# Weight conversion cut into seven steps, 160 steps moved between VectorE and ScalarE, and the step list written anew

## The chip, the cores and the metric

The kernel runs on one core of a Trainium2 chip. The metric is the device time of one execution in microseconds. The kernel before takes 520.02 us, the median of three runs (519.7 to 520.5). Five engines matter: TensorE (PE; PEld is its weight load), VectorE (DVE), ScalarE (ACT), GpSimd (POOL), and SyncE (SP), which here only issues DMAs.

## The reference

A gated linear attention feeds a feed-forward layer with a squared ReLU:

```
B, H, S, D = 4, 8, 768, 48
for t in range(S):
    state = alpha[:, :, t, :, None] * state + einsum('bhd,bhe->bhde', k[:, :, t], v[:, :, t])
    y[:, :, t] = einsum('bhd,bhde->bhe', q[:, :, t], state)
x = y.transpose(0, 2, 1, 3).reshape(B * S, H * D)      # 3072 x 384
h = maximum(x @ w_in, 0)                               # w_in 384 x 2048
out = h * h @ w_out                                    # w_out 2048 x 384
```

The two weight matrices arrive as 64-bit floats, everything else as 32-bit floats. [...]

## The kernel before, in words

**Attention.** The sequence is cut into 24 blocks of 128 positions (6 chunks of 4 batches; block n is chunk n // 4 of batch n % 4). For each block the logarithm of alpha is summed along the positions by a matmul with a triangular matrix (steps `ln`, `log_high`, `log_rest`, `cs`), the sums are exponentiated (`eb`, `ei`), q and k are scaled by them (`mq`, `mk`), turned by TensorE (`qT`, `kT`; from block 4 on `turned_one`) and copied out of PSUM (`qc`, `kc`; from block 4 on `half_copied`, four to a block). Then come the scores (`sc`), the masked copy (`one_masked`), the sums for the state (`kv`), the state update on VectorE (`us`, `sa`, `sb`) and the output of two blocks at a time (`y_states`, `y_inner`, `yb`). Twelve copies of strips (`moved`) carry the output of two blocks to `xT`, the transposed input of the feed-forward layer.

**Feed-forward.** Four blocks make a group of 512 tokens, of which there are six. For the first group part of the first product is made with plain 32-bit matmuls (`ha`, `hb`, `hf`, with `ra`/`qa` and the like for ReLU and square). Everything else is made in three passes of a faster 32-bit format (fp32r): each operand is split into a high part and a rest (`split_x`, `rest_x`, `diff_x` for x; `cast_w`, `rest_w`, `diff_w` for weights; `split_h`, `rest_h`, `diff_h` for the hidden layer), and `in_x` and `in_y`, or `out_x` and `out_y`, multiply them. `out_plain` is the plain 32-bit form of the second product for a group's first pieces. Between the passes the accumulator is scaled (`in_scaled`, `out_scaled`), summed (`in_added`, `out_added`), rectified (`in_post`) and squared (`in_square`). A hidden piece has one of three kinds, A, M and D, which say how it is finished: kind D is finished by one VectorE instruction in `in_post`, kind A is squared on ScalarE, kind M on VectorE. Split weights that do not stay in SBUF are written to DRAM (`kept_l`, `kept_d`) and read back (`fetch`, 144 times).

**Weights.** The matrices are loaded and converted in 16 parts, parts 0 to 7 of `w_in` and 8 to 15 of `w_out`, each 128 x 768 values. A part is loaded by one DMA of 768 KB (`load_weights`, L395 and L399). `first` makes two VectorE instructions (exponent field, L422; upper mantissa bits, L426), `middle` two ScalarE instructions (exponent moved up, L435; lower word scaled, L438), `second` three VectorE instructions (sign, L444; mantissa joined, L448; product, L451).

**Order.** All of it is written out by hand as a list of words, `ORDER`, such as `ha:1` or `moved:0:3:2`. The program walks the list and issues each step's instructions. Each engine executes its own instructions in the order of the list; DMAs are issued in that order by SP, and a DMA that must wait holds up all later ones. Loads of the blocks 4 to 7 and of `w_in` also wait for the newest matmul listed ahead of them. `warm` is a matmul whose result is thrown away; there are 16. All matmuls are recorded at line L350, the ScalarE copies of `moved` at L779, the splits of x and of the hidden layer at L845, `in_scaled` at L898 and L900, `in_post` of kinds A and M at L923, `in_square` at L930 or, like other VectorE additions and products, at L802.

## Time and profile before

| | before |
|---|---|
| median of three runs | 520.02 us |
| profiled execution, its own time | 521.08 us |
| span of the profiled execution | 519.3 us |
| TensorE busy | 508.6 us, 5404 instructions |
| VectorE busy | 362.6 us, 629 instructions |
| ScalarE busy | 314.4 us, 681 instructions |
| HBM read and written | 88.10 MB and 17.33 MB |

The profiled execution takes 1.78 us more than its span, and 1.06 us more than the median. A busy share is an average over stages: what one stage is limited by is read from the stretch of time in which it lies. Instructions of one engine overlap a little at their ends, so that the busy time is less than the sum of the durations.

### The profile page before, as it was taken

What the parts mean: (1) busy time and instruction counts of PE and PEld (TensorE: products, weight loads), DVE (VectorE), ACT (ScalarE), POOL (GpSimd) and SP (SyncE); (2) the same over time, 40 slices, a digit from 0 to 9 for tenths busy, and PEclk for the clock granted to TensorE, in tenths of its full rate; (3) what the DMA queues carried; (4) which work ended last, traced back from release to release, by engine and by line L of the source; (5) the groups of instructions that cost most, each with busy time, mean ns of one, the idle gap of its engine ahead of it and who ended that gap; (6) DMA issues with size and microseconds to landing.
All of it is one profiled execution on the core that took longest, in us unless ns stands there. A gap on an engine that the chain in (4) does not pass through costs nothing.

```text
span 519.3 us, 13138 instructions
## 1 busy us (share of the span) xinstructions
PE 508.6 (98%) x5404; PEld 432.0 (83%) x5404; DVE 362.6 (70%) x629; ACT 314.4 (61%) x681; POOL 5.4 (1%) x29
## 2 busy tenths in 40 slices
PE   8989999999999999999999999999999999999997
PEld 6676788567778879987899988899987899988997
DVE  3678999998988898635998147597344598126961
ACT  4789999977486673058766247765253775324620
POOL 4000000000000000000000000000000000000000
PEclk9989999999999999999999999999999999999999
DMA  9969898977756668698876479756883744579301
GB/s 161 218 174 249 176 266 269 275 236 217 220 170 196 193 219 255 215 308 199 239 185 184 146 230 287 216 153 174 221 259 124 231 136 143 182 273 404 123 0 61
DMA packets 140762, 106.27 MB, mean 205 GB/s; under 512 B 109968, under 2 KB 113056, under 8 KB 140704
## 3 DMA queue, kind: packets, MB, share of 16 engines
q1 hardware_dynamic: 140704, 105.45, 70.1%
q8 instruction: 42, 0.69, 0.6%
q14 instruction: 16, 0.13, 0.1%
HBM read 88.10 MB, written 17.33 MB: 203 GB/s over the span
## 4 chain that ended last, share of the span: by engine, by line
PE 88%; DVE 4%; ACT 3%; DMA 2%; issue 1%; POOL 0%; DVEq 0%; ACTq 0%; POOLq 0%
PE o L350 40%; PE h L350 36%; PE sckv L350 4%; PE y L350 4%; PE cs L350 2%; PE T L350 2%; DMA a_in<-in_alpha_dram 1%; PE warm L350 1%; DMA q_in<-in_q_dram 1%; ACT x L779 1%; DVE hid L802 1%; DVE power L444 1%; DVE w_out L451 0%; DVE w_in L451 0%; DVE w_out L448 0%
## 5 line engine op out<-in xcount | busy, mean ns | idle before, releaser
L350 PE MATMUL h<-xa,wb 128*128 128x512 f32 x264 | 76.4, 397 | 0.8 <-ACT ks L754 0.6
L350 PE MATMUL h<-xl,wl 128*128 128x512 f32 x264 | 74.5, 390 | 0.0
L350 PE MATMUL h<-xd,wd 128*128 128x512 f32 x264 | 69.6, 397 | 0.0
L779 ACT COPY x<-y 32x256 f32<-32x256 f32 (+3 forms) x144 | 50.9, 366 | 16.9 <-PE y L350 14.6
L350 PEld LDWEIGHTS h<-xa,wb 128*128 128x128 f32 x264 | 48.8, 188 | 12.3 <-ACT ks L754 1.0
L350 PEld LDWEIGHTS h<-xl,wl 128*128 128x128 f32 x264 | 49.6, 188 | 11.0 <-DVE xl L848 0.2
L350 PEld LDWEIGHTS h<-xd,wd 128*128 128x128 f32 x264 | 48.7, 188 | 11.0 <-ACT h L900 0.5
L802 DVE TENSOR_TENSOR hid<-h,hid 128x512 f32<-128x512 f32 x44 | 29.7, 687 | 40.2 <-PE h L350 40.1
L350 PE MATMUL o<-wb,ha 128*128 128x384 f32 x168 | 56.9, 339 | 0.1
L350 PE MATMUL o<-wd,hd 128*128 128x384 f32 x320 | 56.9, 334 | 0.0
L350 PE MATMUL o<-wl,hl 128*128 128x384 f32 x168 | 56.2, 335 | 0.0
L350 PEld LDWEIGHTS o<-wd,hd 128*128 128x128 f32 x320 | 55.7, 188 | 0.3
L350 PE MATMUL o<-wb,hx 128*128 128x384 f32 x152 | 51.2, 337 | 0.0
L350 PE MATMUL o<-wl,hx 128*128 128x384 f32 x152 | 50.8, 334 | 0.0
L898 ACT ACTIVATE hid<-h 128x512 f32<-128x512 f32 x44 | 26.3, 598 | 38.8 <-PE h L350 38.7
L923 ACT ACTIVATE hid<-h 128x512 f32<-128x512 f32 x44 | 25.8, 598 | 36.4 <-PE h L350 36.1
L802 DVE TENSOR_TENSOR osb<-o,osb 128x384 f32<-128x384 f32 x24 | 12.9, 555 | 44.7 <-PE o L350 30.9
L350 PE MATMUL o<-w_out,hid 128*128 128x384 f32 x128 | 44.0, 491 | 0.0
L845 ACT ACTIVATE ha<-hid 128x512 fp32r<-128x512 f32 x42 | 26.1, 632 | 22.4 <-DVE hid L918 12.0
L900 ACT ACTIVATE h<-h 128x512 f32<-128x512 f32 x44 | 25.6, 591 | 22.8 <-PE h L350 22.6
L350 PEld LDWEIGHTS o<-w_out,hid 128*128 128x128 f32 x128 | 23.7, 189 | 15.9 <-DVE w_out L451 1.0
L848 DVE SCALAR_TENSOR_TENSOR hl<-ha,hid 128x512 fp32r<-128x512 f32 x42 | 28.3, 686 | 12.1 <-ACT ha L845 11.9
(113 smaller groups left out, 893.2 us busy)
## 6 DMA issues: line engine op xcount, KB each, us to landing
wd<-do SPq DMA_DIRECT2D x38, 384.0 KB
wd<-di SPq DMA_DIRECT2D x36, 384.0 KB
wl<-li SPq DMA_DIRECT2D x36, 384.0 KB
wl<-lo SPq DMA_DIRECT2D x34, 384.0 KB
raw<-in_moe_w_in_dram SPq DMA_DIRECT2D x8, 768.0 KB
raw<-in_moe_w_out_dram SPq DMA_DIRECT2D x8, 768.0 KB
v_in<-in_v_dram SPq DMA_DIRECT2D x24, 192.0 KB
out_dram<-osb SPq DMA_DIRECT2D x24, 192.0 KB
```

The source lines that it names most:

```text
L350: newest[:] = [f(*args, **kwargs)]
L444: nc.vector.scalar_tensor_tensor(out=power, in0=hi, scalar=0x80000000, in1=power, op0=ALU.bitwise_and, op1=ALU.bitwise_or,)
L779: copy(out=xT[g][kk].rearrange("a (t c) -> a t c", c=C)[to : to + m, t : t + 2], in_=blk[n]["y"][e][r : r + m, :, p // 2],)
L802: nc.vector.tensor_tensor(out=o, in0=x, in1=z, op=op)
L845: nc.scalar.activation(out=a, in_=x, func=AF.Copy, scale=NEAR * E)
L848: nc.vector.scalar_tensor_tensor(out=l, in0=a.bitcast(FP32), scalar=-1.0 / E, in1=x, op0=ALU.mult, op1=ALU.add)
L898: nc.scalar.activation(out=hid[j], in_=x, func=AF.Copy, scale=E)
L900: nc.scalar.activation(out=x, in_=x, func=AF.Copy, scale=1.0 + E)
L923: nc.scalar.activation(out=h, in_=acc.pop(("h", j)), func=AF.Relu)
```

## The change

Four things change.

1. `load_weights` becomes `part_loaded`, and `first`, `middle` and `second` become seven steps of one instruction each: `exponent`, `mantissa`, `signed`, `joined`, `valued` on VectorE, `moved_up` on ScalarE, and `lower` on ScalarE (or VectorE). The list can place each by itself.
2. Each of these steps has a second number: 2 means the whole part, 0 or 1 one half of its columns. Parts 0 and 1 of `w_in` are loaded and converted in halves, so that there are 18 loads and 18 of each step instead of 16.
3. A word that ends in `~` runs on the other of VectorE and ScalarE. There are 160: `moved` 32, `split_h` 29, `in_scaled` 23, `in_square` 19, `half_copied` 16, `in_post` 14, `out_scaled` 12, `log_high` 5, `lower` 3, `cast_w` 2, `split_x` 2, and one each of `qc`, `kc` and `out_moved`. Of them 146 go from ScalarE to VectorE, and 14 of `in_square` (kind M) from VectorE to ScalarE.
4. The list is made anew. Apart from the conversion steps it holds the same words as before with the same numbers: the same 5404 matmul instructions, 16 of them pairs of `warm`, the same 96 loads and 144 fetches, in another order.

```diff
-    def load_weights(i):
+    def part_loaded(i, h):
...
         if i < NW:
-            src = moe_w_in[:, i * DF // NW : (i + 1) * DF // NW]
-            behind_newest(nc.sync.dma_start(out=raw, in_=src.rearrange("(k r) f -> r k f", r=128)))
+            cols = columns(i, h)
+            src = moe_w_in[:, i * DF // NW + cols.start : i * DF // NW + cols.stop]
+            behind_newest(nc.sync.dma_start(out=raw[:, :, cols], in_=src.rearrange("(k r) f -> r k f", r=128)))
...
+    over = [False]
+
+    def copied_to(out, x, scale=1.0, vector=False):
+        if vector == over[0]:
+            if scale == 1.0:
+                nc.scalar.copy(out=out, in_=x)
+            else:
+                nc.scalar.activation(out=out, in_=x, func=AF.Copy, scale=scale)
+        elif scale == 1.0:
+            nc.vector.tensor_copy(out=out, in_=x)
+        else:
+            nc.vector.tensor_scalar(out=out, in0=x, scalar1=scale, scalar2=None, op0=ALU.mult)
+
+    def positive_to(out, x):
+        if over[0]:
+            nc.vector.tensor_scalar(out=out, in0=x, scalar1=0.0, scalar2=None, op0=ALU.max)
+        else:
+            nc.scalar.activation(out=out, in_=x, func=AF.Relu)
+
+    def squared_to(out, x, vector=False):
+        if vector == over[0]:
+            nc.scalar.activation(out=out, in_=x, func=AF.Square)
+        else:
+            nc.vector.tensor_tensor(out=out, in0=x, in1=x, op=ALU.mult)
...
+    def exponent(i, h):
         nc.vector.tensor_scalar(
-            out=power, in0=hi, scalar1=20, scalar2=0x7FF,
+            out=wide("power", i, h), in0=wide("hi", i, h), scalar1=20, scalar2=0x7FF,
             op0=ALU.logical_shift_right, op1=ALU.bitwise_and,
         )
+    def mantissa(i, h):
...
+    def moved_up(i, h):
+        power = wide("power", i, h)
+        nc.scalar.activation(out=power, in_=power, func=AF.Relu, scale=2.0**23, bias=rebias)
+
+    def lower(i, h):
+        w, lo = wide("w", i, h), wide("lo", i, h)
+        if over[0]:
+            nc.vector.tensor_scalar(out=w, in0=lo, scalar1=2.0**-52, scalar2=1.0, op0=ALU.mult, op1=ALU.add)
+        else:
+            nc.scalar.activation(out=w, in_=lo, func=AF.Copy, scale=2.0**-52, bias=1.0)
+
+    def signed(i, h):
...
+    def joined(i, h):
...
+    def valued(i, h):
+        w = wide("w", i, h)
+        nc.vector.tensor_tensor(out=w, in0=w, in1=wide("power", i, h).bitcast(FP32), op=ALU.mult)
...
     for word in ORDER.split():
-        f, *given = word.split(":")
+        f, *given = word.rstrip("~").split(":")
+        over[0] = word.endswith("~")
         steps[f](*(int(x) if x.isdigit() else x for x in given))
```

The start of the two lists, down to the first matmul of the feed-forward layer:

```diff
-load:0:a warm:0 warm:0 warm:0 load:1:a warm:0 ln:0 load:0:q ln:1 warm:0 cs:0 eb:0 load:0:k mq:0 load:1:k cs:1
-ei:0 dl:0 load:0:v qT:0 de:0 warm:0 load:3:a load:1:q mk:0 kT:0 qc:0 kc:0 sc:0 kv:0 load:1:v load:2:a
-one_masked:0:1 load_weights:0 load:2:q load:4:a ei:1 mk:1 one_masked:0:0 eb:1 mq:1 ln:3 us:0 cs:3 ei:3 sa:0
-sb:0 dl:1 kT:1 load:2:k load:5:a kc:1 qT:1 qc:1 sc:1 load:3:q load:3:k kv:1 one_masked:1:0 warm:0 ln:2 cs:2
-ei:2 warm:0 eb:2 one_masked:1:1 load:2:v warm:0 warm:0 eb:3 us:1 y_states:0 y_inner:0 warm:0 mq:2 qT:2 ln:4
-first:0 middle:0 dl:3 load:4:q mk:2 de:1 second:0 cs:4 eb:4 load_weights:1 yb:0 load:4:k load:3:v ei:4 qc:2
-dl:2 kT:2 mk:3 mq:3 ln:5 warm:0 cs:5 de:2 kc:2 sc:2 kv:2 one_masked:2:1 moved:0:0:0 warm:0 moved:0:0:1
-moved:0:0:2 mq:4 load_weights:2 moved:0:1:0 kT:3 moved:0:1:1 moved:0:1:2 moved:0:2:0 moved:0:2:1 de:3
-moved:0:2:2 moved:0:3:0 qT:3 moved:0:3:1 moved:0:3:2 one_masked:2:0 us:2 sa:2 sb:2 load:7:a ha:1 ha:0 bl:4
+warm:0 warm:0 load:0:a ln:0 warm:0 cs:0 warm:0 ei:0 load:0:k mk:0 warm:0 load:1:a load:0:q kT:0 load:1:k ln:1
+eb:0 mq:0 load:0:v load:2:a load:3:a cs:1 ei:1 load:1:q part_loaded:0:0 dl:0 qT:0 mk:1 kc:0 qc:0~ de:0 sc:0
+kv:0 ln:2 cs:2 one_masked:0:0 ln:3 one_masked:0:1 load:1:v load:4:a part_loaded:0:1 eb:1 dl:1 kT:1 de:1 mq:1
+load:2:k qT:1 qc:1 kc:1~ cs:3 sc:1 load:2:q load:3:k warm:0 us:0 sa:0 eb:2 eb:3 load:3:q sb:0 exponent:0:0
+kv:1 one_masked:1:0 one_masked:1:1 ei:2 dl:2 load:5:a part_loaded:1:0 warm:0 us:1 exponent:0:1 mk:2 load:2:v
+y_states:0 y_inner:0 yb:0 mantissa:0:0 moved:0:0:0 kT:2 moved:0:0:1 ln:4 lower:0:0~ ei:3 cs:4 warm:0 load:4:q
+joined:0:0 mq:2 load:4:k moved_up:0:1 signed:0:1 load:3:v part_loaded:1:1 moved_up:0:0 eb:4 signed:0:0
+valued:0:0 mk:3 dl:3 warm:0 de:2 mq:3 de:3 bl:4 warm:0 moved:0:0:2 mantissa:0:1 lower:0:1 joined:0:1 load:6:a
+part_loaded:2:2 moved:0:1:0 moved:0:1:1 warm:0 moved:0:1:2~ part_loaded:3:2 ln:5 moved:0:2:0 kc:2 exponent:1:0
+qT:2 kT:3 cs:5 load:7:a valued:0:1 kc:3 moved:0:2:1 qc:2 warm:0 load:5:q moved:0:2:2~ moved:0:3:0~
+moved:0:3:1~ qT:3 qc:3 sc:2 kv:2 load:5:k one_masked:2:0 moved:0:3:2 ei:4 ha:1 ra:1 warm:0 load:4:v
```

## The prediction

> **What bounds the kernel now.** I read the page's head first, then the busy shares in slices and the chain of work that ended last.

> ```profile
> span 519.3 us, 13138 instructions
> ...
> PE 508.6 (98%) x5404; PEld 432.0 (83%) x5404; DVE 362.6 (70%) x629; ACT 314.4 (61%) x681; POOL 5.4 (1%) x29
> ...
> PE   8989999999999999999999999999999999999997
> ...
> DVE  3678999998988898635998147597344598126961
> ACT  4789999977486673058766247765253775324620
> ...
> PEclk9989999999999999999999999999999999999999
> ...
> PE 88%; DVE 4%; ACT 3%; DMA 2%; issue 1%; POOL 0%; DVEq 0%; ACTq 0%; POOLq 0%
> ```

> TensorE is the bound: 98% busy and 88% of the chain. The change makes the same 5404 matmuls, so it can win only what TensorE loses: 519.3 - 508.6 = 10.7 us of idle time, and what it loses inside busy time. The slices show where: early, where VectorE and ScalarE stand at 9 tenths too. So I cut the span at five matmul steps found in both lists (the first `ha:1`, then `y_states` 6, 10, 14 and 20) and at the last matmul's end, and asked for busy time by stretch.

> ```profile
> core 0: us, PE busy (x) PEld busy (x) DVE busy (x) ACT busy (x) POOL busy (x), PEclk, DMA share, GB/s
> 0.00:29.04 29.04, 24.25 (x423) 17.85 (x423) 14.97 (x31) 18.52 (x45) 5.36 (x29) 1.00 1.03 192
> 29.04:87.50 58.46, 57.25 (x813) 44.79 (x811) 53.08 (x93) 53.39 (x121) 0.00 (x0) 0.97 0.86 225
> 87.50:177.60 90.10, 89.29 (x882) 65.41 (x881) 80.61 (x132) 64.82 (x133) 0.00 (x0) 1.00 0.73 214
> 177.60:261.00 83.40, 83.40 (x955) 71.67 (x958) 61.60 (x111) 50.15 (x112) 0.00 (x0) 1.00 0.81 242
> 261.00:394.90 133.90, 133.76 (x1443) 121.44 (x1436) 81.28 (x149) 73.94 (x165) 0.00 (x0) 1.00 0.71 206
> 394.90:516.00 121.10, 120.62 (x925) 110.79 (x915) 70.46 (x116) 53.58 (x109) 0.00 (x0) 1.00 0.48 168
> 516.00:519.30 3.30, 0.00 (x0) 0.00 (x0) 0.56 (x1) 0.00 (x0) 0.00 (x0) 1.00 0.17 60
> ```

> TensorE idles 29.04 - 24.25 = 4.8 us ahead of `ha:1`, 1.2 us in the second stretch, 0.8 in the third, 0.6 in the next three together, and 3.3 at the end. The chain, taken for the first 62 us, says on whom it waits:

> ```profile
> 1.10 4.37 PE warm L350 x10
> ...
> 18.49 0.53 ACT a_in L500
> 19.01 0.83 ACT power L435
> ...
> 27.07 0.37 ACT x L779
> ...
> 27.85 0.66 PE kT L350 x4
> ...
> 29.25 4.19 PE h L350 x12
> ...
> 36.66 2.59 PE h L350 x12
> ...
> 39.92 5.02 DMA q_in<-in_q_dram
> ...
> 46.39 0.88 DVE w_in L448
> ...
> 52.36 0.96 DVE w_in L451
> 54.11 0.46 PE T L350 x8
> ```

> From 18.49 to 27.85 the chain runs mostly through ScalarE (logarithm, conversion, strips), from 45 to 54 through VectorE (conversion of a weight part, ahead of which q and k wait in the same queue). The same 12 matmuls take 4.19 us after TensorE had waited for ScalarE, and 2.59 later: 1.6 us lost to a lower clock, whence the 0.97. So the early stretches offer about 4.8 + 1.2 + 1.6 = 7.6 us, of which the 1.1 us ahead of the first `warm` belong to the program's start.

> **The change, part by part.** Durations are from the groups of instructions, shapes kept apart:

> ```profile
> L779 ACT COPY x<-y 32x256 f32<-32x256 f32 x72 | 26.4, 366 | 16.1 <-PE y L350 14.6
> L898 ACT ACTIVATE hid<-h 128x512 f32<-128x512 f32 x44 | 26.3, 598 | 38.8 <-PE h L350 38.7
> L845 ACT ACTIVATE ha<-hid 128x512 fp32r<-128x512 f32 x42 | 26.1, 632 | 22.4 <-DVE hid L918 12.0 <-DVE hid L802 6.9 <-PE o L350 2.1
> L754 ACT COPY ks<-T 128x256 f32<-128x256 f32 x40 | 14.4, 389 | 2.0 <-PE T L350 1.9
> L802 DVE TENSOR_TENSOR hid<-h,hid 128x512 f32<-128x512 f32 x44 | 29.7, 687 | 40.2 <-PE h L350 40.1
> L548 DVE TENSOR_TENSOR k_in<-k_in,inv 128x384 f32<-128x384 f32 x23 | 12.7, 553 | 0.4 <-DMA k_in<-in_k_dram 0.3
> L422 DVE TENSOR_SCALAR power<-raw 128x768 uint32<-128x768 uint32 x16 | 8.9, 555 | 0.7 <-DMA raw<-in_moe_w_in_dram 0.7
> L448 DVE SCALAR_TENSOR_TENSOR w_in<-upper,w_in 128x768 f32<-128x768 uint32 x8 | 7.6, 954 | 0.0
> L451 DVE TENSOR_TENSOR w_in<-w_in,power 128x768 f32<-128x768 f32 x8 | 7.7, 958 | 0.3
> L438 ACT ACTIVATE w_in<-raw 128x768 f32<-128x768 uint32 x8 | 7.4, 923 | 0.0
> ```

> *Conversion.* Seven instructions a part as before. Two-source rows of 384, 512 and 768 columns (553, 687, 954 ns) give 0.15 us fixed and 1.05 ns a column, so a half part's two-source instruction takes 0.55 and its one-source ones (555 ns for 768) 0.36. Halving two parts adds five VectorE instructions each, 10 x 0.15 = 1.5 us, and the three `lower` that move about 1.9: VectorE +3.2 by exact sums, ScalarE -0.8. Two more DMAs cost SP some 0.5 us each, against 0.37 to 1.0 for others, with transfers behind them anyway: nothing while SP has lead; 1 us if the next q or k is late, as the 5.02 us piece shows that one can be.

> *The 160.* VectorE copies with one source do not stand in the trace at these shapes. From SBUF (`split_h`, `split_x`, `log_high`, `cast_w`) I bound 512 columns between the one-source rate of L422, 0.15 + 512 x 0.53 ns = 0.42 us, and the two-source row, 0.69; L422 also reads SBUF with one source, so I take 0.42. From PSUM (100 steps) the same two ends hold; L802 reads PSUM and takes 0.687, so I take the slow end: a strip 0.42 against 0.366 on ScalarE, a half copy 0.42 against 0.389, `in_scaled` 0.69 against 0.598. ScalarE loses 67.6 us and VectorE gains 65.7; with the conversion VectorE's durations go from 401 to 469 us, ScalarE's from 356 to 289. With SBUF at the slow end VectorE gets 10 us more, with PSUM at the fast end 20 less.

> [...]

> *The order.* I add up, list by list, durations of the steps between the five cuts, less 0.07 us an instruction for overlapping ends (L448 lasts 0.954 and holds the chain 0.88). Before -> after, in us; the bracket has SBUF copies at the slow end:

> | from | ScalarE | VectorE |
> |---|---|---|
> | start to `ha:1` | 16.5 -> 15.0 | 12.4 -> 14.3 |
> | to `y_states:6` | 57.6 -> 53.4 | 58.2 -> 56.6 |
> | to `y_states:10` | 64.0 -> 62.8 | 79.5 -> 84.2 (85.5) |
> | to `y_states:14` | 47.3 -> 36.4 | 62.2 -> 71.9 (73.9) |
> | to `y_states:20` | 72.4 -> 52.8 | 79.8 -> 115.4 (118.9) |
> | to the end | 52.2 -> 30.8 | 68.8 -> 72.6 (75.8) |

> Priced against the stretches:

> (a) To `ha:1`: the chain is ScalarE's, which has 1.5 us less ahead; VectorE has 1.9 more, but is busy 14.97 of 29.04 us. -1.5 us; bounds -3.7 (4.8 less the start's 1.1) and +1 (late loads: the new list puts 2:k ahead of 2:q, and `mk:2` now stands ahead of the first `mantissa` and `joined`, so VectorE's whole queue waits for that load, and TensorE's `kT:2` with it).

> (b) To `y_states:6`: all three engines are nearly full (57.25, 53.08 and 53.39 of 58.46), and the chain changes between the two others. ScalarE is relieved by 4.2 us, VectorE by 1.6; TensorE's visible losses are 1.2 + 1.6 = 2.8. I take -2.5, nearer to the visible loss; bounds -4.2 and +0.3 (VectorE's 1.9 us of earlier work not hidden in its idle time, less its 1.6).

> (c) To `y_states:10`: VectorE is busy 80.61 of 90.10 and gets 4.7 more, so its spare time falls from 9.5 to 4.8 us. The chain already waits there:

> ```profile
> 121.21 1.55 DVE wd L826 x2
> ...
> 150.91 0.88 DVE w_out L448
> ...
> 516.01 0.56 DVE osb L802
> ```

> Steps cut finer can step aside for urgent ones. I take +1.2, a quarter of 4.7; bounds -0.8 (all idle gone) and +4.7 (none absorbed).

> (d) From there to `y_states:20`: VectorE goes from 142 to 187 us in 217. TensorE idles 0.14 now; at the loss of stretch (c), 0.81 in 90 us, it would be 2.0. I take +0.5; bounds -0.1 and +1.8.

> (e) The end keeps its order: `out_y`, a VectorE sum, a store. The 3.3 us behind the last matmul (sum at 516.01, then the store) stay: 0.

> Sum: -1.5 - 2.5 + 1.2 + 0.5 = -2.3 us. The profiled span becomes 517.0; that execution took 521.08, 1.06 above the median of 520.02, so against the median I get 517.7.

> **Rivals.**
> R1, slower: VectorE becomes the bound between 87 and 395 us. For it: 85 us of VectorE work for 90.10 us in (c), and later 142 -> 187. Against: there it works from finished accumulators, with leads of microseconds, and ScalarE is freer. It decides once (c) absorbs less than 1.2 of the 4.7 us (-4.0 + 3.5 + 0.5 = 0): -4.0 + 4.7 + 1.8 = +2.5, 522.5 us.
> R2, little changed: the new start waits. `kT:2`, now right behind `yb:0`, needs 2:k on VectorE; TensorE idles near 18 us and the first `h` matmuls run slowly again. Then (a) gives nothing, (b) loses its 1.6 of clock, and (c) and (d) stay: 0 - 0.9 + 1.7 = +0.8, 520.8. For it: the slow matmuls before followed such a wait, of 1.54 us.

> ```profile
> 27.85 0.66 PE L350 MATMUL kT<-ident,qk_lent 128*128 128x128 f32 x4 [1.54 <-ACT last L573]
> ```

> Against: eight steps and five `warm` lie between that `kT:2` and `ha:1`, in which the clock can come back. [...]
> R3, no change: TensorE's work is the same, and other waits take the place of those removed: 520.0. For it: three engines are near full to 87 us, so what one gives up another takes. Against: ScalarE's 4.2 us less in (b).
> R4, faster still: finer placing removes all of TensorE's visible loss: -3.7 - 2.8 - 0.8 - 0.1 = -7.4, 512.6. For it: each lost stretch waits for a queue whose order is now free. Against: the loads, and 4 us more for VectorE in (c).

> **How the numbers follow.** Forecast 0.46 (own range 515 to 519), R1 0.30, R2 0.08, R3 0.08, R4 0.08. The measurement tells 0.2%, about 1.0 us, from no change. Faster is the forecast and R4: 0.54. Within 0.2%: R3 and half of R2, 0.12. Slower: R1 and the other half, 0.34. The predicted time is 517.7. The range runs from R4, less 0.6 of spread between runs, 512.0, to R1 with (c)'s SBUF copies at the slow end, 522.5 + 1.3, plus 0.7 of spread: 524.5.

> **What would show it.** (a) right: the first `h` matmul starts near 27.5 us instead of 29.04. (b): `y_states:6` near 83.5 instead of 87.50, the PEclk above 0.97 in that stretch. (c), (d): VectorE's busy time near 425 us, ScalarE's near 255; idle TensorE in 87 to 395 released by DVE means R1. A row for VectorE's PSUM strips settles its bounds (0.29 or 0.42), one for `split_h` the other (0.42 or 0.69). The prediction is wrong if the early waits move to a load, or if VectorE's wait time grows more than ScalarE's relief.

## The result, and the profile after

The change makes the kernel slower: 525.79 us, the median of six runs (522.11 to 528.64), against 519.38 us of the kernel before beside it (518.54 to 520.50). The ratio is 1.0111 with a 95% interval of 1.0067 to 1.0156. The forecast was 517.7 us.

The page of the kernel after, its head, three rows of slices, the clock and the shares of the chain:

```profile
span 519.7 us, 13162 instructions
...
PE 506.5 (97%) x5404; PEld 431.2 (83%) x5404; DVE 420.9 (81%) x771; ACT 257.5 (50%) x553; POOL 5.3 (1%) x29
...
PE   7999899999999999999999999999999999999997
...
DVE  4789998899998997976998478998568999446981
ACT  4679899885756644134762134532213635213500
...
PEclk9999999999999999999999999999999999999999
...
PE 85%; ACT 7%; DVE 3%; DMA 2%; SPq 1%; issue 1%; POOLq 0%; ACTq 0%
```

TensorE still bounds. Its busy time is 2.1 us less than in the profile before, and it idles 13.2 us instead of 10.7. One thing has to be known before the two profiles are laid side by side: the profiled execution before, 521.08 us, was one of its longest, and the profiled one after, 522.11 us, is the shortest of its six. The pair shows 1.0 us of a difference that the medians put at 6.4. So beside the profile before I use that of the run `e5_old_list` below (the old list of steps, 519.91 us for its profiled execution), which is a usual one. The pair after and `e5` still shows only 1.6 us by its spans (519.7 and 518.1); a second trace of the kernel after, `e1_after_again` below, shows 3.2 (521.3).

The same cuts as in the prediction, in the kernel after (first matmul of `ha:1`, then `y_states` 6, 10, 14, 20, and the last matmul's end):

```profile
core 0: us, PE busy (x) PEld busy (x) DVE busy (x) ACT busy (x) POOL busy (x), PEclk, DMA share, GB/s
0.00:28.98 28.98, 24.34 (x421) 16.72 (x421) 17.13 (x37) 17.14 (x42) 5.34 (x29) 1.00 1.09 194
28.98:88.46 59.48, 56.71 (x818) 44.18 (x813) 56.38 (x106) 53.35 (x125) 0.00 (x0) 1.00 0.83 222
88.46:178.20 89.74, 88.16 (x880) 66.01 (x879) 83.83 (x137) 61.84 (x124) 0.00 (x0) 1.00 0.70 208
178.20:261.00 82.80, 82.80 (x921) 71.62 (x920) 69.54 (x135) 37.90 (x83) 0.00 (x0) 1.00 0.83 248
261.00:409.20 148.20, 147.62 (x1526) 133.16 (x1529) 117.94 (x225) 54.40 (x119) 0.00 (x0) 1.00 0.70 205
409.20:516.40 107.20, 106.88 (x863) 99.53 (x853) 75.75 (x134) 32.83 (x66) 0.00 (x0) 1.00 0.48 165
516.40:519.70 3.30, 0.00 (x0) 0.00 (x0) 0.35 (x1) 0.00 (x0) 0.00 (x0) 1.00 0.18 63
```

And the first three of them in the old list's usual execution:

```profile
0.00:29.60 29.60, 25.26 (x423) 18.42 (x424) 14.55 (x30) 18.57 (x45) 5.33 (x29) 1.00 1.10 187
29.60:86.60 57.00, 55.87 (x817) 43.42 (x816) 53.64 (x93) 53.21 (x121) 0.00 (x0) 1.00 0.87 232
86.60:176.60 90.00, 89.19 (x880) 65.35 (x879) 80.50 (x132) 64.64 (x133) 0.00 (x0) 1.00 0.73 214
```

The place of the loss, as far as these profiles show it, is the second stretch: 59.48 us against 57.00 (58.46 in the profile before, whose clock was 0.97 there), and 61.0 in `e1_after_again`. The first is 0.6 us shorter, the third 0.3. From `y_states:10` to the end the two lists place `y_states:20` differently, so only the sum compares: 82.80 + 148.20 + 107.20 = 338.2, and 83.40 + 133.90 + 121.10 = 338.4 before. VectorE's much larger load costs nothing there: from `y_states:6` to the last matmul's end the kernel after takes 427.7 us in both of its traces, the old list 428.2.

Inside the second stretch one wait stands out. TensorE's instructions around 62 us, as the timeline of the kernel after has them (start, length, and in brackets the idle time ahead and what ended it):

```profile
61.74 0.55 PE L362 MATMUL y<-am,v_in 64*48 64x64 f32 x22
63.83 0.33 PE L362 MATMUL y<-am,v_in 64*64 64x64 f32 x8 [1.54 <-issue]
```

In the midst of `y_inner:4` TensorE stops for 1.54 us (1.76 from the start of one matmul to that of the next), and "issue" says that no recorded wait explains it. It is the longest wait of the execution, and none like it stands in the old list's.

### The profile page after: what moved, and what is told of

Read it like the earlier page. It is cut to its first block, busy times and chain, and to the rows that moved or that the text cites. A ratio compares the mean times of both kernels' runs of the same rounds, so it can differ in the third digit from the quotient of the medians.

```text
span 519.7 us, 13162 instructions
## 1 busy us (share of the span) xinstructions
PE 506.5 (97%) x5404; PEld 431.2 (83%) x5404; DVE 420.9 (81%) x771; ACT 257.5 (50%) x553; POOL 5.3 (1%) x29
## 4 chain that ended last, share of the span: by engine, by line
PE 85%; ACT 7%; DVE 3%; DMA 2%; SPq 1%; issue 1%; POOLq 0%; ACTq 0%
PE o L362 38%; PE h L362 35%; PE sckv L362 4%; PE y L362 4%; ACT x L421 3%; PE T L362 2%; PE cs L362 1%; DMA raw<-in_moe_w_in_dram 1%; SPq L388 1%; DMA a_lent<-in_alpha_dram 1%; DVE power L494 1%; ACT hid L433 1%; ACT power L483 0%; ACT ha L423 0%; DVE power L471 0%
## 5 line engine op out<-in xcount | busy, mean ns | idle before, releaser
L362 PE MATMUL h<-xa,wb 128*128 128x512 f32 x264 | 75.4, 394 | 0.0
L362 PE MATMUL h<-xl,wl 128*128 128x512 f32 x264 | 74.6, 391 | 0.0
L362 PE MATMUL h<-xd,wd 128*128 128x512 f32 x264 | 70.7, 399 | 0.5 <-ACT h L423 0.4
L421 ACT COPY x<-y 32x256 f32<-32x256 f32 (+3 forms) x112 | 39.8, 365 | 41.1 <-PE y L362 21.7
L362 PEld LDWEIGHTS h<-xd,wd 128*128 128x128 f32 x264 | 48.6, 188 | 12.5 <-ACT h L423 1.6
L362 PEld LDWEIGHTS h<-xl,wl 128*128 128x128 f32 x264 | 49.5, 188 | 10.9 <-DVE wl L865 0.3
L362 PEld LDWEIGHTS h<-xa,wb 128*128 128x128 f32 x264 | 49.0, 188 | 9.9
L362 PE MATMUL o<-wd,hd 128*128 128x384 f32 x320 | 57.0, 334 | 0.0
L362 PE MATMUL o<-wb,ha 128*128 128x384 f32 x168 | 56.6, 337 | 0.0
L362 PE MATMUL o<-wl,hl 128*128 128x384 f32 x168 | 56.3, 335 | 0.0
L362 PEld LDWEIGHTS o<-wd,hd 128*128 128x128 f32 x320 | 55.7, 188 | 0.2
L362 PE MATMUL o<-wb,hx 128*128 128x384 f32 x152 | 51.5, 339 | 0.0
L362 PE MATMUL o<-wl,hx 128*128 128x384 f32 x152 | 50.8, 334 | 0.0
L362 PE MATMUL o<-w_out,hid 128*128 128x384 f32 x128 | 43.6, 489 | 0.7 <-DVE w_out L507 0.7
L852 DVE TENSOR_TENSOR hid<-h,hid 128x512 f32<-128x512 f32 x44 | 30.0, 687 | 16.2 <-PE h L362 16.1
L362 PEld LDWEIGHTS o<-w_out,hid 128*128 128x128 f32 x128 | 23.9, 189 | 16.0 <-DVE w_out L507 1.3
L423 ACT ACTIVATE hid<-h 128x512 f32<-128x512 f32 x30 | 17.8, 597 | 38.7 <-PE h L362 36.6
L423 ACT ACTIVATE h<-h 128x512 f32<-128x512 f32 x35 | 20.4, 588 | 32.7 <-PE h L362 32.0
L433 ACT ACTIVATE hid<-h 128x512 f32<-128x512 f32 x30 | 17.8, 598 | 32.3 <-PE h L362 29.8
L362 PEld LDWEIGHTS o<-wb,ha 128*128 128x128 f32 x168 | 31.5, 188 | 0.5
L362 PEld LDWEIGHTS o<-wl,hl 128*128 128x128 f32 x168 | 31.5, 188 | 0.4
```

Of the source, the lines that this page charges most:

```text
L362: newest[:] = [f(*args, **kwargs)]
L421: nc.scalar.copy(out=out, in_=x)
L423: nc.scalar.activation(out=out, in_=x, func=AF.Copy, scale=scale)
L433: nc.scalar.activation(out=out, in_=x, func=AF.Relu)
L852: nc.vector.tensor_tensor(out=o, in0=x, in1=z, op=op)
```

## The experiments

I count TensorE's matmuls as the trace lists them, from 0, and call them entries; a throw-away matmul makes two. The kernels of the runs have the list in fewer lines, so that their line numbers are lower: L314 or L312 is the matmul line, L362 in the kernel after. Ratios are to the kernel before, run beside on the same chip. Runs of one table row are medians with lowest and highest.

**Which part of the change costs the time?**

The kernel after once more, with no edit:

> The changed kernel as it is, for the spread of its runs and for the profile of another execution. Its first profile has a span of 519.7 us, no more than before (519.3), while its median is 525.8 us with runs from 522.1 to 528.6. Theory C (clock): waits of TensorE in the first 100 us let the granted clock fall in some executions and not in others; then runs spread over 522 to 529 us again, and a slower execution's profile has a mean clock of 0.99 to 0.997 and its extra time in slices with a clock under 1. Theory V (R1 of the prediction, VectorE as the bound after 87 us): extra time after 87 us, spread over it, at full clock. Theory L (loads): the extra time is waits for loads issued late by SP, at full clock.

The new list with no swaps between VectorE and ScalarE:

```diff
-kc:0 qc:0~ de:0 sc:0
+kc:0 qc:0 de:0 sc:0
...
-kT:2 moved:0:0:1 ln:4 lower:0:0~ ei:3
+kT:2 moved:0:0:1 ln:4 lower:0:0 ei:3
...
```

> The new list with every ~ left out: all 160 steps go back to their own engine, the order stays. Theory V: VectorE is back at some 375 us busy, and the time falls to 519 to 521 us. Theories C and L: the start is as it was or worse, since ScalarE, which bounds the start, gets its strips back: 524 to 532 us.

The old list down to the first `y_states:4`, then the new one:

```diff
-warm:0 warm:0 load:0:a ln:0 warm:0 cs:0 warm:0 ei:0 load:0:k mk:0 warm:0 load:1:a load:0:q kT:0 load:1:k ln:1
...
+load:0:a warm:0 warm:0 warm:0 load:1:a warm:0 ln:0 load:0:q ln:1 warm:0 cs:0 eb:0 load:0:k mq:0 load:1:k cs:1
...
```

> The old list's steps up to the first y_states:4 (some 60 us; whole weight parts, no swaps), then the remaining steps in the order of the new list with their swaps. Theories C and L (the new start is at fault): 518 to 521 us with a spread under 2 us. Theory V: 523 to 528 us.

The reverse, the new list down to there and then the old one:

> The new list's steps up to the first y_states:4 (halves and swaps included), then the remaining steps in the order of the old list, without swaps. Theories C and L: 523 to 528 us with a spread over 3 us, as the changed kernel. Theory V: 518 to 521 us.

At the seam `e3` has 14 steps, and `e4` two, that the list followed up to there has only later.

The old list throughout, written in the seven new steps, with whole parts and no swaps:

```diff
-first:0 middle:0 dl:3 load:4:q mk:2 de:1 second:0
+exponent:0:2 mantissa:0:2 moved_up:0:2 lower:0:2 dl:3 load:4:q mk:2 de:1 signed:0:2 joined:0:2 valued:0:2
```

> The old list in the new code: first, middle and second written out as their seven steps in the old places, whole parts, no swaps. It shows what the code itself costs, and gives a second profile of the old order (the one at hand ran at a mean clock of 0.997, its span 519.3; other executions have spans near 517). All theories: the same as before within 0.3%, 518 to 520 us. If the new step code were at fault: 523 us or more.

The new list with parts 0 and 1 whole:

```diff
-load:1:q part_loaded:0:0 dl:0
+load:1:q part_loaded:0:2 dl:0
...
-load:4:a part_loaded:0:1 eb:1
+load:4:a eb:1
...
```

> The new list with parts 0 and 1 of w_in loaded and converted whole: the two loads at the place of the first half's, each conversion step at the place of the second half's. It takes away two DMAs from SP's first 26 us and 10 VectorE instructions. Theory L with the halves at fault: 521 to 523 us. Otherwise 525 to 528 us (the first half can no longer be converted early).

| run | us | ratio, interval |
|---|---|---|
| `e1_after_again` | 525.26 (522.23 to 526.45) | 1.0103, 1.0077 to 1.0129 |
| `e2_no_swaps` | 538.10 (536.82 to 539.40) | 1.0358, 1.0334 to 1.0383 |
| `e3_old_head` | 523.01 (521.56 to 524.11) | 1.0067, 1.0046 to 1.0087 |
| `e4_new_head` | 523.59 (521.86 to 524.69) | 1.0076, 1.0050 to 1.0102 |
| `e5_old_list` | 519.45 (518.55 to 520.62) | 1.0004, 0.9992 to 1.0017 |
| `e8_whole_parts` | 526.45 (523.35 to 530.58) | 1.0145, 1.0103 to 1.0186 |

The new steps themselves cost nothing (`e5`). The swaps do not cost the time either: this list needs them, and is 12.8 us slower without (swaps in the old order were not tried). That speaks against theory V. Halves and whole parts are not told apart. So it is the order. `e3` keeps 3.5 us of the loss although it starts as the old list does, which theories C and L did not expect, but it also waits 1.66 us for a copy at 60.91 us, at the seam of its two lists, so it doesn't show what the rest of the new list costs alone. The stop at 62 us stands in `e1` (1.76 us idle), `e2` (2.72), `e4` (1.55) and `e8` (2.47), after the very same entry, 974, in each, and not in `e3`, which has the old order there.

The second trace of the unchanged kernel also shows what the stop can do. Stretches of 2 us of `e1`, columns as above:

```profile
62.00:64.00 2.00, 0.24 (x14) 0.16 (x13) 1.61 (x4) 1.47 (x5) 0.00 (x0) 1.00 0.55 70
64.00:66.00 2.00, 2.00 (x44) 1.90 (x41) 0.82 (x3) 0.10 (x1) 0.00 (x0) 0.57 0.03 8
66.00:68.00 2.00, 2.00 (x7) 1.58 (x6) 2.00 (x5) 1.50 (x3) 0.00 (x0) 0.58 0.85 170
```

Behind an idle time of 1.76 us the granted clock averages 0.57 and 0.58 over these 4 us (it is 0.50 from 64.27 to 67.68 us); behind the 1.54 us of the kernel after it stays at 1.00. From `y_states:4` to `turned_one:8` this execution takes 9.6 us, the profiled one of after 7.8. So a stop can cost twice, which is one reason why the executions of this list lie so far apart. The length of the stop alone doesn't decide it: in the profile before the clock fell behind an idle time of 1.54 us, too, and in `e7` below it stayed at 1.00 behind 2.06 us.

**Is it a late load, or a clock gone slow?** The load of v for chunk 6 moved ahead of the load of weight part 5:

```diff
-joined:4:2 part_loaded:5:2 turned_one:5
+joined:4:2 load:6:v part_loaded:5:2 turned_one:5
...
-load:7:q load:6:v rb:5
+load:7:q rb:5
```

> The new list with one word moved: load:6:v goes ahead of part_loaded:5:2 and part_loaded:6:2, two loads of 768 KB, instead of behind them. In the profiles of the new list TensorE stops for some 2 us ahead of kv:6, which reads that tile, near 62 us, and the slow clock follows in some executions. Theory L: the stop goes, the time falls by 1.5 to 3 us to 522 to 524 us. Theory C alone (the stop is not for the load): 525 to 526 us. Theory V: 525 us, nothing changes.

Eight more throw-away matmuls at three waits of the early part:

```diff
-ei:3 cs:4 warm:0
+ei:3 warm:1 cs:4 warm:0
...
-moved:2:0:2 ha:5 bl:5
+moved:2:0:2 warm:1 ha:5 bl:5
...
-log_high:9 kv:6 one_masked:6:0
+log_high:9 warm:3 kv:6 one_masked:6:0
```

> The new list with eight more throw-away matmuls where TensorE waits early: two ahead of the first cs:4, two ahead of ha:5, four ahead of kv:6 (in one bank each). They add no work where TensorE waits anyway. Theory C: the clock stays at 1.0 in nearly all executions and the time falls to 521 to 523 us. Theories L and V: the waits stay as long and the time stays at 525 to 526 us, with a clock nearer to 1.0.

`e6` takes 523.29 us (520.98 to 525.63), ratio 1.0077 (1.0051 to 1.0102), but its stop is unchanged, 1.54 us idle at entry 974: the stop doesn't wait for that load. `e7` takes 525.79 us (524.91 to 526.94), ratio 1.0134 (1.0110 to 1.0157); the granted clock was 1.0 on average in three of its four executions, and the time no better. The clock follows the stop, it is not the cause; an execution of `e1` that took 525.99 us had a mean clock of 1.00 as well. The stop of `e7`, 2.06 us idle, stands at entry 974 again, though 8 of its 16 new entries are ahead of it.

**Does TensorE wait for its instructions?** The page lists a DMA queue of its own kind:

```profile
q8 instruction: 42, 0.69, 0.6%
```

These are 42 packets of 16 KB, and TensorE executes 10,808 matmul and weight-load instructions (5404 of each): if the packets bring these, 257 a packet. In the kernel after, one packet starts at 61.42 us and ends at 62.42; TensorE resumes at 63.83. The run of short matmuls around it (`turned_one:7`, `y_states:4`, `sc:6`, `y_inner:4`, `kv:6`: 176 entries some 14 ns apart) passes such a packet's 128 entries (half of 257) in about 2 us. To test this, three runs move the run of short matmuls or the stream of instructions. First `hf:7`, six long matmuls, moved into the run:

```diff
-mk:7 hf:7 load:8:a
+mk:7 load:8:a
...
-load:9:q y_inner:4 sa:5
+load:9:q hf:7 y_inner:4 sa:5
```

> The new list with one word moved: the six long matmuls of hf:7 stand between sc:6 and y_inner:4, in the middle of the run of short matmuls, instead of ahead of it. Theory F (instructions): TensorE's next block of instructions is asked for about one block (128 matmuls with their weight loads) ahead, and takes longer to come than 128 short matmuls last; the run of 176 short matmuls from turned_one:7 to kv:6 outruns it. Then the stop of 1.75 to 2 us at matmul 974 goes, since hf:7's 2.7 us lie in between, and the run gains 1.5 to 2 us: 523.5 to 524, ratio to before 1.007 to 1.009. Theory L (a load or a copy that y_inner:4 waits for): the stop of 1.7 us stays ahead of y_inner:4 or kv:6, or shrinks by hf:7's length only because hf:7 is put into it, and kv:6 starts as late as in the kernel after; time as there, 525.5, ratio 1.011 to 1.013.

Then throw-away matmuls at the very start, which shift all later instructions in the stream (`short` holds the number, here 24, or 100 for the old list):

```diff
     def warm(_):
-        matmul(
-            out=ps_att.tile([128, NP, 64], FP32, tag="att", name="warm"),
-            lhsT=s_t[0].rearrange("a p d -> a (p d)")[:, 0:128], rhs=s_t[0], start=True, stop=True,
-        )
+        t = ps_att.tile([128, NP, 64], FP32, tag="att", name="warm")
+        w = s_t[0].rearrange("a p d -> a (p d)")[:, 0:128]
+        for _ in range(short.pop() if short else 0):
+            matmul(out=t[:, 0, 0:1], lhsT=w, rhs=s_t[0][:, 0, 0:1], start=True, stop=True)
+        matmul(out=t, lhsT=w, rhs=s_t[0], start=True, stop=True)
```

> The new list unchanged, with 24 throw-away matmuls of one column ahead of the first one, in time in which TensorE has nothing to do: all later instructions stand 24 matmuls further on in its stream. F: the end of the block that was at matmul 974 falls 24 matmuls earlier in the work, the request for the next block falls before hf:7, and the stop near 62 us goes or is under 0.6 us; 523.5 to 524, ratio 1.007 to 1.009, though there are more instructions. L: nothing changes, stop of 1.7 us at the same work, ratio 1.011 to 1.013.

> The old list written in the seven new steps (519.45 us, no stop near 60 us), with 100 throw-away matmuls of one column ahead of the first one. F: the block's end is moved into the run of 176 short matmuls that this list has too (y_states:4 to kv:6), so a stop of 1 to 2 us appears between 58 and 62 us, and the time is 520.5 to 521.5, ratio 1.003 to 1.005. L: no stop, 519.5, ratio 0.999 to 1.001.

The same 24 with the earlier load of `e6`:

> The new list with the 24 short matmuls and with the load of v for chunk 6 issued ahead of the copy from DRAM of part 5 (the latter alone: 523.29 us, ratio 1.0077). If the two losses are separate, they add up: 521.5 to 522, ratio 1.004 to 1.006. If what the earlier load gave was the same stop by chance of the executions, 523 to 523.5, ratio 1.007. Under either the new list stays slower than the list before, so that a second cause remains; faster than 519.5 would say that the stop and the late load are all that the new list loses.

| run | us | ratio, interval |
|---|---|---|
| `e9_hf7_later` | 525.80 (522.70 to 529.30) | 1.0132, 1.0094 to 1.0170 |
| `e10_short_24` | 545.73 (543.92 to 546.96) | 1.0505, 1.0484 to 1.0527 |
| `e11_old_short_100` | 581.67 (580.38 to 583.36) | 1.1202, 1.1181 to 1.1224 |
| `e12_both` | 543.27 (542.77 to 546.82) | 1.0475, 1.0450 to 1.0499 |

The stops did what theory F says, and the times didn't. `e9` has no stop at entry 974, but `turned_one:7`, whose wait `hf:7` had covered, now waits 2.79 us from one matmul to the next (2.57 us idle, put down to ScalarE's `power`), the clock is 0.50 for 6.8 us behind it, and nothing is won. In `e10` the stop at 62 us is gone, too. But a throw-away matmul of one column is two entries, not one, and not cheap with 128 columns of weights: 0.21 us an entry at the start. So `ha:1` begins at 43.8 us, 14.8 late, in `e10` (10.3 us of throw-away matmuls; a stop of 1.7 us idle at entry 345 and 10.2 us at a clock of 0.50 behind it are most of the rest), and at 71.1 us in `e11`. That is why `e10`, `e11` and `e12` miss their forecasts by some 20, 60 and 20 us. The shift is 48 and 200 entries. What is left is the finding: in both runs new stops of 1.1 to 3.2 us appear, in `e10` at entries 1478, 3251, 3757, 4265, 4772, in `e11` at 1358, 1611, 2498, 3005, 3385, 3892. Their distances, 253, 380, 506, 507, 508, 887 and 1773, are all multiples of 126.7. Two more, at 2872 in `e10` and 2117 in `e11`, end between long matmuls and fit the same spacing; `e12`, shifted as `e10`, stops at the same entries as `e10`.

**The stream shifted at little cost.** The same with one column of weights, 6 for the new list (12 entries) and 37 for the old one (74):

```diff
-            matmul(out=t[:, 0, 0:1], lhsT=w, rhs=s_t[0][:, 0, 0:1], start=True, stop=True)
+            matmul(out=t[0:1, 0, 0:1], lhsT=w[:, 0:1], rhs=s_t[0][:, 0, 0:1], start=True, stop=True)
```

> The new list unchanged, with 6 throw-away matmuls of one column by one column (12 entries in the trace, two for each) ahead of the first one. The stops of 1.3 to 3.2 us that no wait explains stood, in the run with 24 and in that with 100 throw-away matmuls, 507 entries or a multiple of 126.7 apart in TensorE's order, whatever the work there. F: in the kernel after, one such place is entry 974, at the end of 127 short entries that take 2.2 us; 12 entries earlier in the work the 127 entries before the place take in a part of hf:7. So the stop at 62 us goes or is under 0.6 us, turned_one:8 starts 1.5 us earlier after y_states:4 (after: 7.8 us, here 6.3), and no other stop over 1 us takes its place, 12 entries being too few to move another place into a short run; time 523 to 524, ratio to before 1.007 to 1.009. L (the stop is a wait for data): stop of 1.7 us before the same work, 525.5.

> The old list in the seven new steps, with 37 throw-away matmuls of one column by one column (74 entries). F: by the spacing of 126.7 entries the places stand as in the run with 100 (200 entries, 1.58 spacings), so stops of 1 to 3 us appear near the entries 1232, 1486, 1990, 2372, 2880, 3260 and 3766, and from ha:1 to the end the kernel takes 10 to 15 us more than the old list without them (488.5 us there); whole time 530 to 537, ratio 1.02 to 1.035. L: from ha:1 to the end as without, within 1 us, and at most the start is later by the length of the throw-away matmuls (2 to 4 us).

> The new list with the 6 small matmuls and with the load of v for chunk 6 issued ahead of the copy from DRAM of part 5. F with the late loads as the rest: 521 to 522, ratio 1.004 to 1.006; if the earlier load gave nothing of its own, as the run with 6 small ones alone; at 519.5 or below the stop and that load would be all that the new list loses.

`e14` takes 540.93 us (537.12 to 543.99), ratio 1.0418 (1.0381 to 1.0456): 37 tiny matmuls make the unchanged old list 21 us slower. They delay `ha:1` by 0.9 us; from there to the last matmul's start `e14` takes 507.8 us, the old list 484.8. TensorE's waits by what ended them, in `e14` (total, times, longest):

```profile
PE sckv L312 <- issue: 9.0, 4, 2.9
PE y L312 <- issue: 5.0, 3, 2.9
PE T L312 <- issue: 1.5, 1, 1.5
PE kT L312 <- ACT last L582: 1.5, 1, 1.5
```

and the longest in the old list without the 37:

```profile
PE kT L312 <- ACT last L579: 1.5, 1, 1.5
PE warm L312 <- POOL s L270: 1.1, 1, 1.1
PE sckv L312 <- ACT ks L371: 0.7, 1, 0.7
```

Eight stops with 15.5 us, where there was none, at entries 1230, 1483, 1989, 2370, 2877, 3257 and 3764 (forecast were 1232, 1486, 1990, 2372, 2880, 3260 and 3766) and a short one at 4143. Part of the rest is the clock behind them, as in the two stretches behind the stop at 188 us:

```profile
190.00:192.00 2.00, 1.30 (x9) 0.94 (x10) 0.89 (x2) 1.95 (x6) 0.00 (x0) 0.78 0.50 107
192.00:194.00 2.00, 2.00 (x4) 1.01 (x3) 2.00 (x4) 0.32 (x1) 0.00 (x0) 0.50 0.41 149
```

No work, no data and no order of the old list had changed, so a wait for data cannot explain these stops. And in the five of the table each stop ends 1.35 to 1.46 us after a packet of the instruction queue:

| run, entry | packet, us | TensorE resumes | after the packet's end |
|---|---|---|---|
| after, 974 | 61.42 to 62.42 | 63.83 | 1.41 |
| `e14`, 1230 | 68.85 to 69.78 | 71.24 | 1.46 |
| `e14`, 1483 | 92.57 to 93.96 | 95.39 | 1.43 |
| `e14`, 2370 | 188.39 to 189.32 | 190.70 | 1.38 |
| `e14`, 2877 | 249.41 to 250.88 | 252.23 | 1.35 |

In the traces of all runs I find 46 stops of over 0.7 us among short matmuls with this mark, and the time from the packet's end to the next matmul is 1.2 to 1.7 us in each. Eight more, between long matmuls, have it too, and no idle time of that size put down to "issue" lacks it. That TensorE stops for its instructions is shown.

`e13` is a miss in part: 523.16 us (519.66 to 525.03; an eighth execution, which the ratio leaves out, took 530.60), ratio 1.0067 (1.0042 to 1.0092), as forecast, but the stop in its profile is longer (2.46 us, not under 0.6), at entry 974 again, which is now 12 entries earlier in the work. That it stays at the entry and not with the work is F's mark; a true wait, that of an `o` matmul for the weights at entry 1443 of after, stands at entry 1455 in `e13`. But its packet came at 61.83 us, no earlier than in the kernel after (61.42), though it should have been asked for ahead of most of `hf:7`. `e15` takes 524.83 us (521.61 to 526.46), ratio 1.0104 (1.0080 to 1.0128), with a stop of 2.61 us and its packet at 62.0: the earlier load adds nothing, and what `e6` had won stays unsettled.

**Why is the packet late?** The DMA engines' mean share is in the last column but one; the kernel after again, by 2 us:

```profile
54.00:56.00 2.00, 2.00 (x62) 1.72 (x54) 2.00 (x5) 2.00 (x6) 0.00 (x0) 1.00 0.33 70
56.00:58.00 2.00, 2.00 (x21) 1.24 (x20) 2.00 (x7) 1.97 (x6) 0.00 (x0) 1.00 1.07 208
58.00:60.00 2.00, 2.00 (x15) 0.76 (x15) 2.00 (x6) 2.00 (x5) 0.00 (x0) 1.00 1.20 216
60.00:62.00 2.00, 2.00 (x128) 1.93 (x128) 2.00 (x3) 1.97 (x6) 0.00 (x0) 1.00 1.20 181
62.00:64.00 2.00, 0.46 (x30) 0.33 (x24) 1.82 (x4) 1.67 (x5) 0.00 (x0) 1.00 0.66 89
```

SP issues seven loads in one burst from 54.88 to 60.83 us, and the packet comes when the burst ends. In the old list's execution the packet for this place comes at 57.37 us, during `hf:7`; there SP waits at `bl:7` until 58.38 us, and the share from 58 to 60 us is 0.64. It ends at 58.56 us, and TensorE passes entry 974 at 60.31, 1.75 us later, just late enough not to stop. Two runs thin the burst, the first by smaller loads of q and k for chunks 8 and 9:

```diff
+            hs = slice(0, 1 if n in (8, 9) and x in "qk" else H)
             ins = nc.sync.dma_start(
-                out=t[:, :, 0:D] if x in "qk" else t.rearrange("a (h d) -> a h d", h=H),
-                in_=srcs[x][b, :, c * C : (c + 1) * C, :].rearrange("h s d -> s h d"),
+                out=t[:, hs, 0:D] if x in "qk" else t.rearrange("a (h d) -> a h d", h=H),
+                in_=srcs[x][b, hs, c * C : (c + 1) * C, :].rearrange("h s d -> s h d"),
             )
```

> The new list unchanged; the loads of q and k for chunks 8 and 9 (four of the transfers that SP issues from 57.7 us on) bring one head of eight, so the outputs of these two chunks are not the reference's, and 0.67 MB of DMA are gone. In the kernel after, the instruction packet of TensorE starts at 61.4 us, the DMA engines being busy 1.07 to 1.20 of each 2 us from 56 to 62 us, and TensorE resumes 1.41 us after the packet's end. FQ (the packet queues behind the loads): it starts 1 us or more earlier, at 60.4 or before, the stop at entry 974 shrinks from 1.76 us to under 0.8, and the time falls by 1.5 to 2.5 us to 523 to 524, ratio 1.007 to 1.010. F without queueing (the packet is only asked for too late): packet at 61.4, stop 1.7, time 525.5.

the second by moving two loads of alpha forward:

```diff
-load:7:q load:6:v
+load:8:a load:9:a load:7:q load:6:v
...
-hf:7 load:8:a load:9:a load:8:k
+hf:7 load:8:k
```

> The new list with load:8:a and load:9:a issued ahead of load:7:q instead of behind load:6:v, into the stretch from 54 to 56 us in which the kernel after has the DMA engines busy 0.33. All work is done. FQ: the loads behind them end 1 to 2 us earlier, the instruction packet starts at 59.5 to 60.4 us, the stop at entry 974 is under 0.8 us, and the time is 523 to 524, ratio 1.007 to 1.010. F without queueing: packet at 61.4, stop 1.7 us, 525.5.

and the last adds 8 tiny matmuls (16 entries) to that:

> The run with the two loads of alpha moved out of the burst (523.13 us; stops of 1.19 us at entry 974 and of 0.86 us at entry 2744), with 8 throw-away matmuls of one column by one column (16 entries) ahead of the first one. FQ: the request for the packet falls 16 entries earlier in the work, ahead of all of hf:7 (2.8 us), and behind fewer loads than in the run with 6 small ones alone, so the packet starts at 60 us or before and the stop at entry 974 is under 0.5 us; the stop at entry 2744 (absent with 12 entries) goes; no other stop over 1 us. Time 521 to 522, ratio 1.003 to 1.005: still slower than the kernel before, since the head's many short waits (the 1.0 us ahead of ha:5 at 41 us among them) are left. If the packet is again at 61.5 us or later, as with the 6 small ones, the moment of the request isn't what the throw-away matmuls move, and the time is 523 to 524.

| run | us | ratio, interval | packet starts | stop at 974, start to start |
|---|---|---|---|---|
| `e1_after_again` | 525.26 (522.23 to 526.45) | 1.0103, 1.0077 to 1.0129 | 61.4 | 1.97 |
| `e16_small_loads` | 522.83 (521.81 to 525.97) | 1.0069, 1.0042 to 1.0095 | 60.6 | 0.99 |
| `e17_a89_earlier` | 523.13 (521.87 to 524.25) | 1.0064, 1.0045 to 1.0084 | 61.2 | 1.19 |
| `e18_a89_small_8` | 522.70 (521.66 to 523.87) | 1.0063, 1.0045 to 1.0081 | 57.2 | none |

`e16` came out near its numbers: packet 0.8 us earlier, stop 0.8 us shorter (forecast 1 us and under 0.8 us left). `e17` has the time that was forecast, but the packet is only 0.8 us earlier against `y_states:4` (0.3 us behind its start instead of 1.1) and a stop of 1.19 us is left, where under 0.8 was expected. In `e18` the packet comes four microseconds earlier, and TensorE runs through the place:

```profile
62.44 0.62 PE L314 MATMUL y<-am,v_in 64*48 64x64 f32 x29
62.87 0.23 PE L314 MATMUL sckv<-v_in,k_in 64*64 64x48 f32 x2
62.89 0.23 PE L314 MATMUL y<-am,v_in 64*64 64x64 f32 x2
62.92 0.66 PE L314 MATMUL sckv<-v_in,k_in 64*64 64x48 f32 x30
```

So with less DMA ahead of it the packet came sooner (60.6 us in `e16`, 61.4 in the kernel after), and with an earlier place in the stream as well (57.2 us in `e18`) the stop is gone. That it queues behind the loads fits all of this; the moment at which it is asked for is in no trace, so the queueing is inferred, not seen. The traces narrow it down. In each of the 20, however far its stream is shifted, no packet starts more than 18 to 26 entries ahead of the place one block before the one whose instructions it brings. If it is asked for 24 entries ahead of that place (an estimate from these earliest starts), the packets start 1.1 us later where the DMA engines' share is under 0.05 in the next 1 us (median of 127), and 3.2 us later where it is 0.8 or more (median of 494). `e13` and `e18` pass the entry in question, 823, at the same time, 54.9 us; the packet starts at 61.8 us in `e13` and at 57.2 in `e18`, whose loads of alpha are out of the burst.

Without the stop the new list takes 522.7 us, 2.6 us less than `e1`, and its executions spread over 2.2 us instead of 4.2. It also shows the theory's other side: two new short stops, one of 0.57 us idle at entry 595, and one at entry 3757, where `e10`, `e12` and `e13` had theirs, in the midst of long matmuls:

```profile
312.70 0.39 PE L314 MATMUL h<-xd,wd 128*128 128x512 f32 x1
314.04 0.62 PE L314 MATMUL h<-xd,wd 128*128 128x512 f32 x2 [0.94 <-issue]
```

No version of the new list beats the old one. What is left of the loss, 3.3 us by the medians (522.70 against 519.45 for `e5`), I can place in part: the profiled spans differ by 1.7 us (519.8 and 518.1), about as much as those two stops; the other 1.5 us lie in executions that were not profiled. Their cause stays open. So by these runs the stop at 62 us is worth some 2 to 3 of about 6 us, and for the rest no cause is shown. A list without the run of short matmuls was not tried.

## Why the prediction was wrong

**What it had right.** TensorE bounds in both. The busy sums came out near the forecast, VectorE 420.9 us (425), ScalarE 257.5 (255); but 425 is the total of the forecast's table with its SBUF copies at the slow end, and the durations it chose add up to 415. The prices of the swapped steps were right, too. The rows that had been missing, with shapes kept apart, in the kernel after:

```profile
L427 DVE TENSOR_SCALAR hid<-h 128x512 f32<-128x512 f32 x14 | 9.6, 688 | 6.8 <-PE h L362 6.6
L427 DVE TENSOR_SCALAR ha<-hid 128x512 fp32r<-128x512 f32 x17 | 7.2, 421 | 0.1
L425 DVE COPY x<-y 32x256 f32<-32x256 f32 x15 | 6.4, 424 | 0.7 <-PE y L362 0.3
L425 DVE COPY qs<-T 128x256 f32<-128x256 f32 x11 | 4.4, 417 | 0.5 <-ACT ks L421 0.5
```

688 ns for `in_scaled` (forecast 0.69), 421 for a split from SBUF (0.42), 424 for a strip and 417 for a half copy from PSUM (0.42 each). In the first two rows 512 columns with one source took 688 ns from PSUM and 421 from SBUF.

**Step (b), to `y_states:6`, failed, and is the main error:** -2.5 us forecast, +1.0 by the two profiles (58.46 to 59.48), +2.5 against a usual execution (57.00), and +4.0 if the kernel after is taken from `e1` (61.0). Two things were wrong in it. First, 1.6 of its 2.8 us were a slow clock that not every execution of the old list has: in the profile of `e5`, with a wait of 1.52 us at the same `kT`, it is 1.00 in that stretch, which takes 57.00 us. The forecast took the 1.06 us by which that execution lay above the median off the total, and counted the gain on it all the same. Second, the sums of the two serving engines were taken for the limit, and ScalarE's 4.2 us less for a gain. But TensorE's wait moved to a resource that the sums don't hold, its own instructions: a stop of 1.54 us idle in the kernel after, 1.76 with the slow clock behind it in `e1`. `e18` shows the stretch without the stop at 62 us: 58.7 us, still not under 57.00, so ScalarE's relief did not show as a gain there either; why is open.

**Step (a), to `ha:1`, failed:** -1.5 us forecast, -0.1 measured (-0.6 against `e5`). ScalarE did have less to do (17.14 us busy after 18.52), but the chain of the kernel after begins elsewhere:

```profile
4.57 0.71 SPq L388
5.32 1.03 SPq L388
6.39 4.79 DMA a_lent<-in_alpha_dram
11.20 0.52 ACT a_lent L556
```

SP's issues of the loads and the landing of the third load of alpha at 11.2 us stand there, where the old list's chain has TensorE and ScalarE at work. The forecast named late loads only as its upper bound.

**Step (c)** had the sign wrong: +1.2 forecast, -0.4 measured (90.10 to 89.74). VectorE is busy 83.83 us instead of 80.61 in it, and all of that is absorbed: taking a quarter of VectorE's new work as visible had no ground. **Step (d)** can't be read alone, since `y_states:20` stands elsewhere in the new list; to the end it and (e) together give -0.2. **Step (e)** held: 3.3 us behind the last matmul.

**The rivals.** R1 named the right sign and a wrong place: in the two traces of the kernel after nothing is lost behind `y_states:6`, where VectorE should have become the bound. R2's wait of `kT:2` is small (that group waits 0.5 us in all for VectorE), and the clock holds there (1.00 up to `ha:1`). R3's reason, that other waits take the place of those removed, comes nearest, but the wait that came was of another kind. No rival held TensorE's instructions, and in the profile before nothing marks them but the line of the queue.

The two counts of a block agree: 126.7 entries with a weight load each are 253 recorded instructions between two places, and the queue's 42 packets give 257 a packet. In the kernel after one such place has a stop of over 0.7 us (1.54 us); in `e14` eight stops took 15.5 us of idle time.

## What to carry to other kernels

Where TensorE executed some 128 short matmuls with their weight loads in a row (in 1.8 to 2.1 us, while in the stops behind such runs it resumed 3.0 to 5.4 us after the place before), the place at which the instruction blocks end decided whether it stopped. Of the 54 stops 28 stand behind such runs, the others behind longer blocks, three of them (in `e2`, `e8` and `e9`) behind blocks of 7.3 to 8.3 us. A wait put down to "issue" that ended 1.2 to 1.7 us after a packet of the instruction queue was the mark; 74 entries more at the start brought eight stops (`e14`), 16 more with two loads moved took one away (`e18`), and smaller loads at that time shortened it from 1.97 to 0.99 us (`e16`). So a reorder or an insertion can cost microseconds that no sum over engines shows. The old list has no stop over 0.7 us of this kind, and eight when shifted by 74 entries; that suggests, without showing it, that a kernel tuned by trial has such places tuned in. And price a gain against the usual execution, not against a loss that one profiled execution happened to have.
